# First loads of an attention-plus-MLP kernel: part of them moved to ScalarE's queue, the keys' tails multiplied last

## The chip, the cores and the metric

The kernel runs on one core of a Trainium2 chip. The metric is the device time of one execution in microseconds. An execution is one launch that computes the whole output from inputs in HBM.

## The reference, cut to what matters

There are 8 batches, 8 heads, 576 positions and a head size of 64. `phi` turns the 576 keys and values of a head into 32 "memory" keys and values; the queries attend to those; the result goes through an MLP from 512 to 2048 and back.

```python
a = phi - np.max(phi, axis=2, keepdims=True)
a = np.exp(a)
a = a / (np.sum(a, axis=2, keepdims=True) + 1e-09)
k_m = np.einsum('bhsm,bhsd->bhmd', a, k)
v_m = np.einsum('bhsm,bhsd->bhmd', a, v)
scores = (1.0 / np.sqrt(64)) * np.matmul(q, k_m.transpose(0, 1, 3, 2))
attn = np.exp(scores - np.max(scores, axis=-1, keepdims=True))
attn = attn / (np.sum(attn, axis=-1, keepdims=True) + 1e-09)
x = np.matmul(attn, v_m)        # then (B, S, H * D)
h = x @ w_in
out = (h - np.tanh(h)) @ w_out
```

## The kernel before, in words

The work is one long program written out in a fixed order. The text `START` is a list of words that the loop at its end runs one after the other; each word stands for a step in the table `STEPS`. Each engine then does its instructions strictly in the order of the words (`in_order` ties every instruction to the one ahead of it on its engine). The words of `START` prepare batch 0, convert the weights and lead into the steady part, which goes over 18 tiles of 256 tokens with 4 blocks of hidden units each.

The change touches the first words, those of batch 0:

- `FX0` loads `phi` (tile `pt`, two loads of 288 KB, one for each row of heads, `r` = 0 and 1).
- `KK01`, `KK00` load the keys of row 1 and row 0 (`load_half`, 520 KB each, tiles `kv01` and `kv00`, from `in_kk_dram`). With row 0 come the keys' tails, positions 512 to 575 (tile `kt`, 130 KB, from `in_kkt_dram`).
- `Q00`, `Q01` load the two halves of the queries (`load_q`, 576 KB each).
- `KV00`, `KV01` load the values of row 0 and row 1 (512 KB each, from `in_vv_dram`); with row 0 come the values' tails (128 KB, from `in_vvt_dram`).
- `XR`, `YX`, `XT` take each row's maximum of `phi` on VectorE (line 319), the exponential on ScalarE (line 322, in place in `pt`) and its transposes on TensorE (lines 335 and 336), whose results VectorE and ScalarE copy into tile `e`.
- `VK00`, `VK01` multiply `e` with the keys into `pk` on TensorE (`pool_first`, line 206 for the four full blocks, line 210 for the tails); `VV01`, `VV00` do it with the values later.
- `NK0`, `UK0`, `S00`, `S01`, `AM`, `AE`, `AD`, `AT` divide, transpose, make the scores and the softmax of batch 0.
- `Z00` is a warming pair, two matmuls of ones whose result nobody reads (`warm`, line 969). `N_WARM` such pairs stand ahead of all words.

A load is issued by an engine: SyncE (SP) for most, ScalarE (ACT) for the keys of row 0. The framework gives every load one of eight semaphores, `DMAHW0` to `DMAHW7`, in turn, and puts a wait on an issue that takes a semaphore for the second time: the load that had it before must have landed.

Of the kernel before, what the change touches and what calls it, by code (L numbers as in the profile page):

```python
# [62 lines left out]
        _free.append(P_TAG[_b, _f])  # L63

START = """
FX0 KK01 KK00 Q00 Q01 KV00 XR00 YX00 XT00 XR01 YX01 XT00 XT01 XT01 XT01 Z00 VK00 VK01 Z00 NK0 UK0 UK0 Z00 S00 Z00 S01
S00 AM00 S01 AM01 AM00 KV01 i4:kv2 i2:gg AM01 i3:gg AE00 VV01 Z00 i0:gg AD00 AE01 Z00 Z00 i1:pp5 Z00 VV00 Z00 T02 AD01
Z00 Z00 AD00 NV0 AT00 UU0 i6:kv3 T02 T01 T02 T01 T01 AD01 KB1 AT01 o0:pp5 T02 T00 T01 Z00 T00 L01 T00 T00 Lp02 Lp00
FX1 Lp00 o1:gg L01 UV0 Z00 T03 UV0 T03 T03 AS00 AS01 T03 o6:gg P00 AS00 P00 Lp03 PL00 Lp02 o7:gg Lp03 H00 AS01 P01 T08
H10 XR10 XR11 YX10 XT10 P01 H00 T08 PL01 ap00 YX11 KA1 o3:pp5 H10 o2:gg XT10 XT11 a10 XT11 ap00 T11 XT11 T11 T11 T08  # L70
# [24 lines left out]
N_PLACES = {"gg": 3, "h3": 2, "sm": 2, "sz": 2}  # L95
ENGINES = {name: row[0] for row in ENGINE_LIST.strip().splitlines() for name in row[2:].split()}
W_TAG = "qt us ot qt ot qt pr ot qt pr us ot qt us ot qt".split()
N_WARM = 5
N_CHECK = N_F1 + 2 * B + DF // P + DM // P


# [44 lines left out]
class Attention:  # L146
# [32 lines left out]
    def load_half(self, d, r, kv):  # L179

        n, o = ((65, 0), (64, 1040))[kv]
        src = self.ins[("kk", "vv")[kv]]
        if not kv:
            d["kv0", r] = self.big.tile([P, 2064], F32, tag=f"kv{r}", name=f"kv0{r}", bufs=1)
        t = d["kv0", r][:, o : o + 16 * n]
        queue = self.tc.nc.sync if kv or r else self.tc.nc.scalar
        queue.dma_start(t, src[r])
        for h in range(4):
            d["kv"[kv], h, r] = t.rearrange("p (h c x) -> p h c x", h=4, c=4)[:, h]
        if r == 0:  # L190
            if not kv:
                d["kt0"] = self.big.tile([P, 516], F32, tag="kt", name="kt0", bufs=1)
            t = d["kt0"][:, o // 4 : o // 4 + 4 * n]
            self.tc.nc.sync.dma_start(t, self.ins[("kkt", "vvt")[kv]])
            d["kv"[kv], "t"] = t.rearrange("p (h x) -> p h x", h=4)

    def pool_first(self, d, r, kv):

        nc, e, k = self.tc.nc, d["e"], "kv"[kv]
        if "pk" not in d:  # L200
            d["pk"] = self.psum("pk0")
        d[k, "p"] = pa = d["pk"][:, :, 128:192] if kv else d["pk"][:, :, 0:65]
        for c in range(4):
            for h in range(4):
                hs = slice(32 * h, 32 * h + 32)
                nc.tensor.matmul(pa[hs, r], e[:, c + 4 * r, hs], d[k, h, r][:, c], start=(c == 0), stop=False)
        rs = slice(64 * r, 64 * r + 64)
        for h in range(4):
            hs = slice(32 * h, 32 * h + 32)
            nc.tensor.matmul(pa[hs, r], e[rs, 8, hs], d[k, "t"][rs, h], start=False, stop=True)  # L210

    def norm_first(self, d, kv):
        nc, big, pa = self.tc.nc, self.big, d["kv"[kv], "p"]
# [37 lines left out]

    def load_q(self, b, d, t, tag):
        x = self.big.tile([P, 4, HS], F32, tag=tag, name=f"q{b}{t}", bufs=2 if tag == "q" else 1)
        self.tc.nc.sync.dma_start(x, self.ins["qt"][b, t])
        for h in range(4):
            d["q", h, t] = x[:, h]

# [203 lines left out]
def split_path(ctx, tc, c, ins, out, kept):  # L461
# [502 lines left out]
    def warm(*_):  # L964

        if "z" not in acc:
            acc["z"] = ps_o.tile([P, DM], F32, tag="o0", name="warm")
        for _ in range(2):
            nc.tensor.matmul(acc["z"], c["w16"], c["w16"].unsqueeze(1).to_broadcast((P, 4, P)), start=True, stop=True)
# [51 lines left out]

    for _ in range(N_WARM):
        warm()
# [380 lines left out]
```

## Time and profile before

| | |
|---|---|
| time, median of 3 runs | 639.83 us (639.36 to 640.59) |
| the profiled execution's own time | 639.59 us |
| its span, first to last instruction | 637.8 us |
| TensorE busy | 626.3 us, 98% of the span |
| VectorE, ScalarE, GpSimd busy | 514.8, 366.6, 276.1 us |
| chain of waits | 76% TensorE, 8% VectorE, 6% issue, 4% each GpSimd and ScalarE, 2% DMA |

The span is 1.79 us shorter than the execution's own time, and that execution is 0.24 us faster than the median. Nearly all of the span belongs to TensorE; the first 25 us are where it stands idle most.

### The profile page before, as it was taken

What the parts mean: (1) busy time and instruction counts of PE and PEld (TensorE: products, weight loads), DVE (VectorE), ACT (ScalarE), POOL (GpSimd) and SP (SyncE); (2) the same over time, 40 slices, a digit from 0 to 9 for tenths busy, and PEclk for the clock granted to TensorE, in tenths of its full rate; (3) what the DMA queues carried; (4) which work ended last, traced back from release to release, by engine and by line L of the source; (5) the groups of instructions that cost most, each with busy time, mean ns of one, the idle gap of its engine ahead of it and who ended that gap; (6) DMA issues with size and microseconds to landing.
All of it is one profiled execution on the core that took longest, in us unless ns stands there. A gap on an engine that the chain in (4) does not pass through costs nothing.

```text
span 637.8 us, 15488 instructions
## 1 busy us (share of the span) xinstructions
PE 626.3 (98%) x6656; PEld 452.4 (71%) x6656; DVE 514.8 (81%) x747; ACT 366.6 (57%) x487; POOL 276.1 (43%) x190
## 2 busy tenths in 40 slices
PE   7899999999999999999999999999999999999997
PEld 3374765556567778787867777778787777888886
DVE  5999888779995778875988889888987888858775
ACT  2777887544424555445564565645655576776641
POOL 2467665733042354423443363435432565455530
PEclk9999999999999999999999999999999999999999
DMA  8999750403232403243342432441353333234201
GB/s 337 363 351 412 273 208 34 141 1 134 69 115 105 170 3 108 37 161 136 108 101 93 174 100 55 148 175 39 104 158 142 101 120 113 83 108 126 83 35 38
DMA packets 28300, 85.50 MB, mean 134 GB/s; under 512 B 3648, under 2 KB 4416, under 8 KB 27712
## 3 DMA queue, kind: packets, MB, share of 16 engines
q1 hardware_dynamic: 26928, 81.80, 36.9%
q10 hardware_dynamic: 1296, 2.63, 1.1%
q8 instruction: 54, 0.88, 0.6%
q14 instruction: 22, 0.18, 0.1%
HBM read 72.88 MB, written 11.54 MB: 132 GB/s over the span
## 4 chain that ended last, share of the span: by engine, by line
PE 76%; DVE 8%; issue 6%; POOL 4%; ACT 4%; DMA 2%; POOLq 0%; ACTq 0%; DVEq 0%
PE hs L724 17%; PE x L871 12%; PE o L864 10%; PE o L805 9%; PE o L871 8%; PE h L724 7%; PE o1h L805 3%; PE pp L685 3%; PE pkv L355 2%; POOL g L760 2%; DVE h L749 2%; DVE f L773 2%; ACT u L731 2%; DVE h L739 2%; DMA kv<-in_kk_dram 1%
## 5 line engine op out<-in xcount | busy, mean ns | idle before, releaser
L760 POOL TENSOR_TENSOR g<-h,g 128x1024 f16<-128x1024 f32 x65 | 142.0, 2185 | 296.1 <-ACT g L114 198.7
L724 PEld LDWEIGHTS <-ph 128*128 128x128 f16 x2304 | 177.5, 98 | 18.8 <-issue 4.1
L724 PE MATMUL hs<-ah,ph 128*128 128x256 f16 (+3 forms) x1152 | 151.4, 246 | 0.0
L114 ACT ACTIVATE g<-h 128x1024 f16<-128x1024 f32 x69 | 73.0, 1057 | 102.9 <-DVE h L749 98.8
L724 PE MATMUL hs<-al,ph 128*128 128x256 f16 (+3 forms) x576 | 127.6, 246 | 0.0
L739 DVE SCALAR_TENSOR_TENSOR h<-hs,u 128x1024 f32<-128x1024 f32 x54 | 65.9, 1220 | 72.8 <-ACT u L731 72.1
L744 ACT ACTIVATE u<-u,beta 128x1024 f32<-128x1024 f32 x72 | 82.6, 1149 | 64.0 <-DVE h L739 64.0
L864 PE MATMUL o<-wout_hi,g 128*128 128x512 f16 x432 | 104.6, 379 | 0.0
L871 PEld LDWEIGHTS <-f 128*128 128x128 f16 x896 | 87.7, 98 | 10.1
L749 DVE SCALAR_TENSOR_TENSOR h<-u,h 128x1024 f32<-128x1024 f32 x72 | 88.2, 1226 | 3.5 <-ACT u L744 3.5
L871 PEld LDWEIGHTS <-g 128*128 128x128 f16 x672 | 64.1, 98 | 27.4 <-issue 6.0
L871 PE MATMUL x<-bt,f 128*128 128x256 f16 x672 | 82.5, 273 | 0.0
L731 ACT ACTIVATE u<-hs 128x1024 f32<-128x1024 f32 x54 | 54.8, 1016 | 28.0 <-PE hs L724 25.3
L773 DVE TENSOR_TENSOR f<-g 128x512 f16<-128x512 f16 x112 | 69.3, 659 | 1.7
L864 PEld LDWEIGHTS <-g 128*128 128x128 f16 x432 | 41.2, 98 | 40.2 <-issue 3.8
L805 PEld LDWEIGHTS <-g 128*128 128x128 f16 x384 | 36.6, 98 | 46.5 <-issue 2.6
L805 PE MATMUL o<-wout_hi,g 128*128 128x512 f16 x192 | 58.8, 379 | 0.0
L724 PE MATMUL h<-ah,ph 128*128 128x256 f16 (+3 forms) x384 | 50.0, 246 | 0.0
L724 PE MATMUL h<-al,ph 128*128 128x256 f16 (+2 forms) x192 | 42.5, 246 | 0.0
L805 PE MATMUL o<-wout_lo,g 128*128 128x512 f16 x96 | 36.4, 379 | 0.0
L703 DVE SCALAR_TENSOR_TENSOR ph<-pp,ph 128x1024 f16<-128x1024 f32 x26 | 31.6, 1217 | 4.0 <-ACT ph L114 4.0
L600 POOL TENSOR_TENSOR fy<-chk 128x512 f32<-128x512 f32 x32 | 33.7, 1067 | 0.0
(191 smaller groups left out, 968.7 us busy)
## 6 DMA issues: line engine op xcount, KB each, us to landing
q<-in_qt_dram SPq DMA_DIRECT2D x16, 576.0 KB, 5.6
kv<-in_kva_dram SPq DMA_DIRECT2D x16, 516.0 KB, 6.2
chk<-in_w_in_dram SPq DMA_DIRECT2D x16, 512.0 KB, 5.8
chk<-in_w_out_dram SPq DMA_DIRECT2D x16, 512.0 KB, 3.5
out_dram<-r SPq DMA_DIRECT2D x28, 256.0 KB, 2.4
raws<-in_w_in_dram SPq DMA_DIRECT2D x12, 511.8 KB, 8.3
raw<-in_w_out_dram SPq DMA_DIRECT2D x12, 511.8 KB, 6.6
kv<-in_kva_dram SPq DMA_DIRECT2D x4, 1032.0 KB, 10.3
```

The source lines that it names most:

```text
L114: nc.scalar.activation(o, x, AF.Copy, scale=1.0 if scale is None else scale)
L600: nc.gpsimd.tensor_tensor(y, hf, hf, op=ALU.mult)
L724: nc.tensor.matmul(hp[:, k, tu : tu + w], px[:, g, cs], d[ax][:, g, ta : ta + w], start=(n == 0), stop=(n == 5),)
L731: nc.scalar.activation(uu, hp, AF.Square, scale=1.0 / (S_A * S_P))
L739: nc.vector.scalar_tensor_tensor(h3, hp, C2 * S_G / (S_A * S_P), uu, op0=ALU.mult, op1=ALU.mult)
L744: nc.scalar.activation(uu, uu, AF.Square, bias=c["beta"])
L749: nc.vector.scalar_tensor_tensor(h3, uu, CC, hp, op0=ALU.add, op1=ALU.mult)
L760: (eng or on(nc, f"gl{u}_{fb}", "g")).tensor_tensor(gg[:, 1], h3, gg[:, 0], op=ALU.subtract)
L773: nc.vector.tensor_tensor(o, x, y, op=op)
L805: nc.tensor.matmul(o, gx[:, k, P * tt : P * tt + P], wx[:, 4 * fb + k, :], start=(first and k == 0 and wx is wout_hi and gx is gh), stop=( ...
L864: nc.tensor.matmul(o[th], gg[:, 0, k, P * th : P * th + P], wout_hi[:, 4 * fb + k, :], start=(first and k == 0), stop=False)
L871: nc.tensor.matmul(dst, a(1 - n, kk), b(n, kk), start=(new and kk == 0 and n == 0), stop=(end and kk == 1 and n == 1))
```

## The change

ScalarE's queue issues three more loads: the keys' tails, the second half of batch 0's queries, and the values of row 1. The word `KV01` goes from its place behind the first scores to the head of the list, so that its load is issued next to the others. In `pool_first` the products of the keys' tails for both rows come behind the full blocks of both rows (for the values nothing changes there). `N_WARM` goes from 5 to 6. Lines behind line 205 move by one or none: the exponential is line 323 now, the warming pair 970.

```diff
 START = """
-FX0 KK01 KK00 Q00 Q01 KV00 XR00 YX00 XT00 XR01 YX01 XT00 XT01 XT01 XT01 Z00 VK00 VK01 Z00 NK0 UK0 UK0 Z00 S00 Z00 S01
-S00 AM00 S01 AM01 AM00 KV01 i4:kv2 i2:gg AM01 i3:gg AE00 VV01 Z00 i0:gg AD00 AE01 Z00 Z00 i1:pp5 Z00 VV00 Z00 T02 AD01
+FX0 KK01 KK00 Q00 Q01 KV00 KV01 XR00 YX00 XT00 XR01 YX01 XT00 XT01 XT01 XT01 Z00 VK00 VK01 Z00 NK0 UK0 UK0 Z00 S00 Z00
+S01 S00 AM00 S01 AM01 AM00 i4:kv2 i2:gg AM01 i3:gg AE00 VV01 Z00 i0:gg AD00 AE01 Z00 Z00 i1:pp5 Z00 VV00 Z00 T02 AD01
-N_WARM = 5
+N_WARM = 6
@@ load_half
-        queue = self.tc.nc.sync if kv or r else self.tc.nc.scalar
-        queue.dma_start(t, src[r])
+        (self.tc.nc.scalar if kv == r else self.tc.nc.sync).dma_start(t, src[r])
-            self.tc.nc.sync.dma_start(t, self.ins[("kkt", "vvt")[kv]])
+            (self.tc.nc.sync if kv else self.tc.nc.scalar).dma_start(t, self.ins[("kkt", "vvt")[kv]])
@@ pool_first
-        rs = slice(64 * r, 64 * r + 64)
-        for h in range(4):
-            hs = slice(32 * h, 32 * h + 32)
-            nc.tensor.matmul(pa[hs, r], e[rs, 8, hs], d[k, "t"][rs, h], start=False, stop=True)
+        for i in (r,) if kv else range(2 * r):
+            rs = slice(64 * i, 64 * i + 64)
+            for h in range(4):
+                hs = slice(32 * h, 32 * h + 32)
+                nc.tensor.matmul(pa[hs, i], e[rs, 8, hs], d[k, "t"][rs, h], start=False, stop=True)
@@ load_q
-        self.tc.nc.sync.dma_start(x, self.ins["qt"][b, t])
+        queue = self.tc.nc.scalar if (b, t) == (0, 1) else self.tc.nc.sync
+        queue.dma_start(x, self.ins["qt"][b, t])
```

How this moves instructions is seen in the built programs. The rows below give source line, operation, written tile, read tiles and size; what stands in brackets are the semaphores that an instruction waits for (`DMAHW` of loads, the others of engines).

ScalarE's first instructions, before:

```order
L1345 ACT_TABLE_LOAD
L1345 ACTIVATE exp_66<-one_61 128x1 [waits Pool_49]
L187 DMA kv00_127<-in_kk_dram 128x1040
L322 ACTIVATE pt0_122<-pt0_122,mx00_137 128x576 [waits DMAHW0_49,DVE_49]
L322 ACTIVATE pt0_122<-pt0_122,mx01_148 128x576 [waits DMAHW1_49,DVE_49]
L114 ACTIVATE e0_141<-pet01_152 128x512 [waits PE_49]
```

and now:

```order
L1346 ACT_TABLE_LOAD
L1346 ACTIVATE exp_66<-one_61 128x1 [waits Pool_49]
L186 DMA kv00_129<-in_kk_dram 128x1040 [waits DMAHW0_49]
L193 DMA kt0_131<-in_kkt_dram 128x260 [waits DMAHW2_49]
L255 DMA q01_135<-in_qt_dram 128x1152 [waits DMAHW3_49]
L186 DMA kv01_127<-in_vv_dram 128x1024 [waits DMAHW5_49]
L323 ACTIVATE pt0_124<-pt0_124,mx00_140 128x576 [waits DVE_49]
L323 ACTIVATE pt0_124<-pt0_124,mx01_151 128x576 [waits DMAHW1_49,DVE_49]
L114 ACTIVATE e0_144<-pet01_155 128x512 [waits PE_49]
```

Ahead of the first exponential there were one issue and no wait for a load's semaphore but that of `phi`; now there are four issues, each with a wait for a semaphore of an earlier load.

SyncE's first issues, before:

```order
L164 DMA pt0_122<-in_phx_dram 128x576 x2
L187 DMA kv01_125<-in_kk_dram 128x1040
L194 DMA kt0_129<-in_kkt_dram 128x260
L254 DMA q00_131<-in_qt_dram 128x1152
L254 DMA q01_133<-in_qt_dram 128x1152
L187 DMA kv00_127<-in_vv_dram 128x1024
L194 DMA kt0_129<-in_vvt_dram 128x256 [waits DMAHW0_49]
L187 DMA kv01_125<-in_vv_dram 128x1024 [waits DMAHW1_49]
L494 DMA raws4_245<-in_w_in_dram 128x2047 [waits DMAHW2_49]
L494 DMA raws4_245<-in_w_in_dram 128x2047 [waits DMAHW3_49]
L494 DMA raw2_248<-in_w_in_dram 128x2047 [waits DMAHW4_49]
```

and now:

```order
L164 DMA pt0_124<-in_phx_dram 128x576 x2
L186 DMA kv01_127<-in_kk_dram 128x1040
L255 DMA q00_133<-in_qt_dram 128x1152
L186 DMA kv00_129<-in_vv_dram 128x1024
L193 DMA kt0_131<-in_vvt_dram 128x256
L495 DMA raws4_247<-in_w_in_dram 128x2047 x2
L495 DMA raw2_250<-in_w_in_dram 128x2047 [waits DMAHW1_49]
L495 DMA raw3_253<-in_w_in_dram 128x2047 [waits DMAHW4_49]
```

Three loads left SyncE's list. Its first eight loads now take the semaphores 0 to 7 in the order of the rows: `phi` 0 and 1, the keys of row 1 take 2, the first queries 3, the values of row 0 take 4, the values' tails 5, the first weights (`raws4`) 6 and 7.

TensorE's products with the keys (`pk0` is the accumulator), before:

```order
L206 MATMUL pk0_162<-kv00_127,e0_141 32x65 [waits DMAHW7_49,DVE_49]
L206 MATMUL pk0_162<-kv00_127,e0_141 32x65 x15
L210 MATMUL pk0_162<-kt0_129,e0_141 32x65 [waits DMAHW3_49,DVE_49]
L210 MATMUL pk0_162<-kt0_129,e0_141 32x65 x3
L206 MATMUL pk0_162<-kv01_125,e0_141 32x65 [waits DMAHW2_49,Activation_49]
L206 MATMUL pk0_162<-kv01_125,e0_141 32x65 x15
L210 MATMUL pk0_162<-kt0_129,e0_141 32x65 x4
```

and now, with the first rows of the scores (`psc00`, `psc01`) and of the products with the values behind them:

```order
L205 MATMUL pk0_165<-kv00_129,e0_144 32x65 [waits DMAHW0_49,DVE_49]
L205 MATMUL pk0_165<-kv00_129,e0_144 32x65 x15
L205 MATMUL pk0_165<-kv01_127,e0_144 32x65 [waits DMAHW2_49,Activation_49]
L205 MATMUL pk0_165<-kv01_127,e0_144 32x65 x15
L210 MATMUL pk0_165<-kt0_131,e0_144 32x65 [waits DMAHW2_49,DVE_49]
L210 MATMUL pk0_165<-kt0_131,e0_144 32x65 x7
...
L396 MATMUL psc00_219<-q00_133,kT0_215 32x288 [waits DMAHW3_49,Activation_49]
...
L396 MATMUL psc01_231<-q01_135,kT0_215 32x288 [waits DMAHW3_49]
...
L205 MATMUL pk0_165<-kv01_127,e0_144 32x64 [waits DMAHW5_49]
```

The eight tail products stand together behind the 32 others and the waits name the semaphores of the moved loads: tails 2, second queries 3, values of row 1 semaphore 5, each used a second time.

## Rows read from the trace of the kernel before

**Rows 1.** The page's parts 1 and 4: busy time, and the chain that ended last.

```profile
PE 626.3 (98%) x6656; PEld 452.4 (71%) x6656; DVE 514.8 (81%) x747; ACT 366.6 (57%) x487; POOL 276.1 (43%) x190
...
PE 76%; DVE 8%; issue 6%; POOL 4%; ACT 4%; DMA 2%; POOLq 0%; ACTq 0%; DVEq 0%
```

**Rows 2.** The chain in order of time, first 25 us: start us, us, what.

```profile
1.57 7.06 DMA kv<-in_kk_dram
8.63 0.14 issue
8.77 0.67 PE pk L206 x32
```

**Rows 3.** Timeline of ScalarE (ACT; ACTq is its sequencer): start us, us, what, idle before.

```profile
0.74 1.28 ACT L1345 ACT_TABLE_LOAD   x1 [0.74 <-PEq L1393]
1.57 0.41 ACTq L187 DMA_DIRECT2D kv<-in_kk_dram  x1
2.04 0.20 ACT L1345 ACTIVATE exp<-one 128x1 f32<-128x1 f32 x1
4.54 1.49 ACT L322 ACTIVATE pt<-pt,mx 128x576 f32<-128x576 f32 x2 [2.31 <-DVE mx L319]
```

**Rows 4.** Timeline of TensorE (PE).

```profile
1.06 3.95 PE L969 MATMUL warm<-w 128*128 128x512 f16 x10 [1.06 <-DVE w L1338]
5.42 0.63 PE L335 MATMUL pet<-ident,pt 128*128 128x128 f32 x4 [0.41 <-issue]
7.29 0.61 PE L969 MATMUL warm<-w 128*128 128x512 f16 x2
8.77 0.67 PE L206 MATMUL pk<-kv,e 128*32 128x65 f32 x32 [0.87 <-DMA kv<-in_kk_dram]
10.46 0.60 PE L969 MATMUL warm<-w 128*128 128x512 f16 x2
14.72 0.65 PE L206 MATMUL pk<-kv,e 128*32 128x64 f32 x32 [0.72 <-DMA kv<-in_vv_dram]
```

**Rows 5.** Timeline of SyncE's issues (SPq).

```profile
2.60 0.94 SPq L254 DMA_DIRECT2D q<-in_qt_dram  x2
3.07 0.47 SPq L254 DMA_DIRECT2D q<-in_qt_dram  x1
5.04 0.56 SPq L194 DMA_DIRECT2D kt<-in_vvt_dram  x1
8.84 0.82 SPq L494 DMA_DIRECT2D raws<-in_w_in_dram  x2
```

**Rows 6.** What SyncE's queue waited for, first 16 us: us in total, times, longest.

```profile
SPq L494 <- DMA kv<-in_kk_dram: 2.7, 1, 2.7
SPq L494 <- DMA q<-in_qt_dram: 1.8, 2, 1.1
```

**Rows 7.** Single issues in the DMA view: KB each, us from issue to landing.

```profile
q<-in_qt_dram SPq DMA_DIRECT2D x1, 576.0 KB, 7.8
q<-in_qt_dram SPq DMA_DIRECT2D x1, 576.0 KB, 8.7
kt<-in_vvt_dram SPq DMA_DIRECT2D x1, 128.0 KB, 8.4
```

**Rows 8.** Stretches: us, busy of PE, PEld, DVE, ACT, POOL, PEclk, DMA share, GB/s.

```profile
0.00:2.00 2.00, 0.94 (x3) 0.39 (x4) 0.82 (x3) 1.26 (x1) 1.39 (x12) 1.00 0.11 14
3.00:4.00 1.00, 1.00 (x3) 0.30 (x2) 0.76 (x3) 0.00 (x0) 0.37 (x1) 1.00 1.02 399
8.00:9.00 1.00, 0.23 (x17) 0.26 (x21) 0.00 (x0) 0.00 (x0) 0.00 (x0) 1.00 1.05 418
60.00:640.00 580.00, 572.69 (x6070) 423.48 (x6054) 465.03 (x673) 326.96 (x429) 247.73 (x157) 1.00 0.33 110
```

**Rows 9.** Warming matmuls of the first 5 us, then of 15 to 20 us: ns min/median/max.

```profile
L969 PE MATMUL warm<-w x10: 379/634/634, 1.1 to 4.6; 128*128 128x512 f16 x10
...
L969 PE MATMUL warm<-w x16: 379/379/390, 15.6 to 20.0; 128*128 128x512 f16 x16
```

## The prediction

> **What bounds the kernel now.** I read the page's busy shares and its chain first: TensorE is busy 98% of the span and holds 76% of the chain [rows 1]. The windows say where the other 2% are: from 60 to 640 us TensorE works 572.69 of 580 us [rows 8]. A delay that reaches this part can therefore not be caught up there, and a start that ends earlier is worth nearly its full length. So the question is what ends last in the start. The chain in order of time names it: ScalarE's issue of the keys of row 0 at 1.57, 7.06 us until they have landed at 8.63, and then at 8.77 the first product with the keys [rows 2]. TensorE's timeline agrees: it stood idle 0.87 us ahead of that product, waiting for the keys [rows 4]. Behind 8.77 the chain goes product, VectorE, GpSimd, ScalarE without a load in it, so each later step starts as much later or earlier as this product does.
>
> Two things beside the keys must be done before that product. ScalarE takes the exponentials of `phi` from 4.54 [rows 3]; TensorE's transposes of them start at 5.42, and the warming pair behind the transposes is done at 7.29 + 0.61 = 7.90 [rows 4]. So a product that waited for no load could start 7.90 - 4.54 = 3.36 us behind the start of the first exponential; in this run it had 0.87 us of slack.
>
> **The change part by part.**
>
> *Four issues ahead of the exponentials on ScalarE's queue.* In ScalarE's new list all four loads stand ahead of the first exponential, and each waits for a semaphore that another load used: the keys of row 0 for `phi`'s first load, the tails for the keys of row 1, the second queries for the first queries, the values of row 1 for the values' tails (semaphore 5, the sixth load of SyncE). Nothing in the data asks for that; it comes from eight semaphores going round. That such a wait does hold a queue is seen on SyncE: the weights' load shares no data with the keys, yet its issue stood 2.7 us until the keys of row 1 had landed and went out at 8.84, and two more issues stood 1.8 us behind the queries [rows 5, 6]. Now the same happens on a queue that has arithmetic behind it. The first exponential cannot start before the last of the four is issued, so before the values' tails have landed.
>
> When is that? I count the bytes that go ahead. Before, the first queries landed at 2.60 + 7.8 = 10.4 us with 2322 KB issued up to them, the second at 3.07 + 8.7 = 11.8 with 2898 KB, the values' tails at 5.04 + 8.4 = 13.4 with 3538 KB [rows 5, 7]. That is 1216 KB in 3.0 us, 405 KB in a microsecond, and the windows show the same, 399 to 418 GB/s with all 16 DMA engines busy [rows 8]. Now SyncE has 576 + 520 + 576 + 512 + 128 = 2312 KB up to the values' tails, and ScalarE's queue puts the keys of row 0 and the tails beside them, 650 KB: 2962 KB, which by those rows is 11.8 + 64 / 405 = 12.0 us. If nothing of ScalarE's queue went ahead, it is the 10.4 of 2322 KB; if the second queries went ahead too, it is the 13.4 of 3538 KB. I take 12.0, since ScalarE's two loads are issued early and its second queries only once the first ones are in. The last issue then takes 0.41 us as ScalarE's issue did [rows 3] and the wait some 0.1: the first exponential starts at **12.5 instead of 4.54**. Without a further cost the product starts at 12.5 + 3.36 = 15.9, which is **+7.1 us** against 8.77, between +5.5 and +8.5. Who waits behind it: VectorE's copies of `e`, GpSimd's subtraction of the maxima and SyncE's later loads into tiles that these steps free, all of them by as much.
>
> *TensorE's clock in the gap.* TensorE has nothing to do from the end of the warming pairs (1.06 + 3.95 = 5.0, some 0.4 later with the sixth) until its first transpose at about 13.4. In before it came out of an idle stretch once, at the start: of the first ten warming matmuls most lasted 634 ns, those of 15 to 20 us 379 [rows 9], though the granted-clock column prints 1.00 from the first row on [rows 8]. Ten in 3.95 us [rows 4] is 8 at about 0.43 and 2 at 0.22 apart, so it ran at the lower of its levels (1.2 GHz) first and lost 8 x 0.21 = 1.7 us there. No row shows whether it falls in a gap that comes later. The lower bound is nothing. The upper is that all of TensorE's work from the transposes through the products goes at half speed: (7.90 - 5.42) + (10.46 - 8.77) = 4.2 us more [rows 4]. I take the **1.7** of the start, as the engine comes out of idleness in both. The Trainium skill says (TensorE: Matmul & The Clock Gate, "What's actually happening") that the lower clock is the default and that activity lifts it; by that the term is there, without it the forecast would be 646.7. The start of this trace agrees with it, the gap has no row.
>
> *The tails' products behind the others.* The same 40 products in another order, none added: 0. They read the tails later, which helps only if the tails are the last to land. They are issued when the keys of row 1 have landed, and are among the 2962 KB that are in by 12.0; the products come behind 15.9.
>
> *Loads taken off SyncE.* SyncE reaches the weights sooner: its `raws4` issues wait for nothing now, where they went out at 8.84 [rows 5]. No step of the chain's first 16 us waits for weights, so this is worth 0. TensorE's 0.72 us at 14.72, the wait for the values of row 1 [rows 4], is not in the chain either, which goes over VectorE there; 0. The values of row 1 go out at 12.0 and are wanted some 8.8 us behind 14.72, at 23.5; the longest landing of the rows here is 8.7 [rows 7], which is covered.
>
> *The sixth warming pair.* Two more matmuls, at most 2 x 0.43 = 0.9 us on TensorE ahead of the transposes; the wait for the exponentials covers them. If that cover were gone they would end at 5.4 to 5.9 beside the transposes' 5.42, up to 0.5 us.
>
> **Sum** against the profiled execution's 639.59 us (0.24 below the median of the runs): +7.1 and +1.7 give +8.8, **648.4 us**. The ends of both terms give +5.5 (645.1) and +8.5 + 4.2 (652.3).
>
> **The rivals.**
>
> *The exponentials are not held (the other side).* Then the change does what its words say. The keys wait 0.87 us less, at most: the product starts at 7.90 and the time is 638.7. For it speaks that ScalarE's queue issued its load at 1.57 while its table load ran until 2.02 [rows 3]; issue and arithmetic do overlap. Against it: there the issue ran ahead of work that came earlier in the list; here the exponential would have to overtake an issue that waits. The point that decides is whether the first exponential starts at 4.5. And the tails would then land late, about 9.5 (130 KB behind 520 on ScalarE's queue, issued only when row 1's keys are in), so that most of the 0.87 is lost again: 638.7 to 639.6, or 638.0 at best if TensorE's 0.72 at 14.72 counted too. The Trainium skill goes further (DMA: Bandwidth & Descriptors, "Issuing engines are not separate DMA queues"): loads from several engines share the same 16 DMA engines, and spreading them saves only the time to issue. By that the gain would be nothing, 639.6; the rows with all DMA engines busy agree. Chance 0.04, a quarter of it for the best case.
>
> *Held, but for less.* The eight semaphores' waits end sooner than my count (the values' tails at 10.4 or before) and the clock does not fall: 639.59 + 5.5 = 645.1, or down to 643 if some of the delay is absorbed between 25 and 60 us by loads that are further ahead. No wait for a load stands in the chain there, so I give it 0.12.
>
> *Held, and the clock stays low through the products:* 639.59 + 7.1 + 4.2 = 650.9, or 652.3 with the late landing. Chance 0.14.
>
> *Something later takes all of the delay back,* so that nothing is seen: 639.6. The 572.69 of 580 us speak against it [rows 8]. Chance 0.01.
>
> **How the numbers follow.** The forecast has 0.69, with its own range 646.5 to 650. The range 644.6 to 651.5 takes in most of the two cases beside it and leaves out the not-slower ones and the farthest ends, some 0.12 together. A measurement of this kernel can tell 0.2% (1.3 us) from no change. Slower is all but the first and the last rival: 0.95; faster 0.01, the best case of the first rival; the same 0.04, the rest of it and the last rival.
>
> **What the changed profile would show.** Right: four issues on ScalarE's queue, the last at about 12 us; the first exponential at 12.5; the first product with the keys without a wait for a load, at 16 to 18; matmuls of 634 ns among the first behind the gap; and the same steps from there to the end, 8 to 9 us later. Wrong: an exponential at 4.5, a product with the keys ahead of 10 us, or a last issue on ScalarE's queue that starts early and waits for nothing.

## The result, and the profile after

The changed kernel took 649.25 us (median of 4 runs, 648.83 to 649.73) where the kernel before took 639.66 beside it (4 runs): a ratio of 1.0145, 95% interval 1.013 to 1.0159. It is slower by 9.6 us; the forecast was 648.4, the range 644.6 to 651.5. The profiled execution of the changed kernel took 648.83 us, its span is 647.0: 9.24 more than the profiled execution of before. It is the fastest of the four: its mean granted clock was 0.995, that of the other three 0.992.

The page of the changed kernel, parts 1 and 4, answers to [rows 1]: the chain lost 6 points of TensorE and gained 4 of VectorE and 2 of "issue".

```profile
PE 629.5 (97%) x6658; PEld 453.2 (70%) x6658; DVE 516.3 (80%) x747; ACT 366.1 (57%) x487; POOL 274.7 (42%) x190
...
PE 70%; DVE 12%; issue 8%; POOL 4%; ACT 4%; DMA 2%; SPq 0%; DVEq 0%; POOLq 0%; ACTq 0%
```

The chain in order of time shows the new hole, though not its cause: it calls it "issue", time in which TensorE waited for nothing that the profile shows.

```profile
1.06 5.30 PE warm L970 x12
6.36 6.84 issue
```

The cause stands in ScalarE's timeline of the changed kernel (against [rows 3]) and in two issues of its DMA view (KB each, us from issue to landing):

```profile
3.68 0.39 ACTq L186 DMA_DIRECT2D kv<-in_kk_dram  x1
6.52 0.34 ACTq L193 DMA_DIRECT2D kt<-in_kkt_dram  x1
8.71 0.33 ACTq L255 DMA_DIRECT2D q<-in_qt_dram  x1
11.95 0.33 ACTq L186 DMA_DIRECT2D kv<-in_vv_dram  x1
12.33 1.44 ACT L323 ACTIVATE pt<-pt,mx 128x576 f32<-128x576 f32 x2 [10.09 <-DMA kt<-in_kkt_dram]
```

```profile
kt<-in_vvt_dram SPq DMA_DIRECT2D x1, 128.0 KB, 8.9
kt<-in_kkt_dram ACTq DMA_DIRECT2D x1, 130.0 KB, 6.0
```

Four issues, each late by its semaphore, and then the exponentials at 12.33 instead of 4.54. The last issue went out at 11.95: the values' tails were issued at 3.07 and took 8.9 us to land. The exponentials' row names the keys' tails, the other load into tile `kt`; those landed only at 6.52 + 6.0 = 12.5, so the load that ended the wait is the values' tails. What follows on TensorE (against [rows 4]):

```profile
13.21 1.08 PE L336 MATMUL pet<-ident,pt 128*128 128x128 f32 x4 [6.84 <-issue]
17.36 1.13 PE L205 MATMUL pk<-kv,e 128*32 128x65 f32 x64
18.42 0.34 PE L210 MATMUL pk<-kt,e 64*32 64x65 f32 x16
18.70 0.60 PE L970 MATMUL warm<-w 128*128 128x512 f16 x2
```

The product with the keys starts at 17.36 instead of 8.77 and waits for no load. The windows of the changed kernel (columns as in [rows 8]) say that TensorE worked at half its clock there: 0.50 is 1.2 GHz.

```profile
10.00:12.00 2.00, 0.00 (x0) 0.00 (x0) 0.00 (x0) 0.00 (x0) 0.00 (x0) 0.59 1.05 393
12.00:17.00 5.00, 3.79 (x14) 2.14 (x14) 0.98 (x2) 2.04 (x3) 0.00 (x0) 0.50 1.02 414
17.00:18.00 1.00, 1.00 (x46) 0.64 (x48) 0.00 (x0) 0.00 (x0) 0.00 (x0) 0.91 1.01 410
```

To follow the delay further I take one late step of the start as a marker: GpSimd's second subtraction of the maxima in batch 0. In the kernel before:

```profile
16.05 1.16 POOL L425 TENSOR_TENSOR sc<-sc,sm 128x576 f32<-128x576 f32 x1 [0.31 <-DVE sm L423]
```

and in the changed one:

```profile
24.32 1.16 POOL L426 TENSOR_TENSOR sc<-sc,sm 128x576 f32<-128x576 f32 x1 [0.31 <-DVE sm L424]
```

The delay is 8.59 us at the first product, 8.27 at the marker (in the new order the products take 1.34 us, 17.36 to 18.70, where they took 1.69, 8.77 to 10.46 [rows 4]) and stays between 8.2 and 8.5 up to about 180 us. Then it grows by 0.73 in one place. VectorE's subtraction `bt` and GpSimd's subtraction `al` start within 20 ns of each other there, and one of them takes twice its time. In the kernel before, GpSimd's row and then VectorE's:

```profile
178.61 2.37 POOL L676 TENSOR_TENSOR al<-af,ah 128x576 f16<-128x576 f32 x1 [0.99 <-ACT ah L114]
...
178.63 1.21 DVE L787 TENSOR_TENSOR bt<-wout_lo 128x2048 f16<-128x2048 f16 x1
```

and the same two in the changed kernel:

```profile
187.02 1.28 POOL L677 TENSOR_TENSOR al<-af,ah 128x576 f16<-128x576 f32 x1 [0.99 <-ACT ah L114]
...
187.04 2.34 DVE L788 TENSOR_TENSOR bt<-wout_lo 128x2048 f16<-128x2048 f16 x1
```

I read the durations so: before, VectorE went first and GpSimd stood; now GpSimd went first and VectorE, which has more queued behind it, stood. From there the delay is 9.1 to 9.2 us to the end, but for single steps.

### The profile page after: what moved, and what is told of

The parts are those of the page before. It is cut to its first block, busy times and chain, and to the rows that moved or that the text cites. A ratio compares the mean times of both kernels' runs of the same rounds, so it can differ in the third digit from the quotient of the medians.

```text
span 647.0 us, 15491 instructions
## 1 busy us (share of the span) xinstructions
PE 629.5 (97%) x6658; PEld 453.2 (70%) x6658; DVE 516.3 (80%) x747; ACT 366.1 (57%) x487; POOL 274.7 (42%) x190
## 4 chain that ended last, share of the span: by engine, by line
PE 70%; DVE 12%; issue 8%; POOL 4%; ACT 4%; DMA 2%; SPq 0%; DVEq 0%; POOLq 0%; ACTq 0%
PE hs L725 16%; PE x L872 12%; PE o L865 9%; PE o L872 8%; PE h L725 6%; PE o L806 6%; PE o1h L806 3%; PE pp L686 2%; DVE h L750 2%; PE pkv L356 2%; DVE h L740 2%; DVE f L774 2%; ACT u L732 2%; POOL g L761 2%; DMA pt<-in_phx_dram 1%
## 5 line engine op out<-in xcount | busy, mean ns | idle before, releaser
L872 PE MATMUL o<-bt,g 128*128 128x256 f16 x224 | 33.6, 273 | 0.0
```

The costliest lines, as they stand in the source:

```text
L872: nc.tensor.matmul(dst, a(1 - n, kk), b(n, kk), start=(new and kk == 0 and n == 0), stop=(end and kk == 1 and n == 1))
```

## The experiments

Theory: ScalarE's queue is held by issues that wait for a reused semaphore, so the exponentials come late; the low clock behind the gap adds 1.7 us. Rivals: the loss comes from the loads as such (bytes on a second queue, another order of the transfers); it comes from the values of row 1 issued early, or from the order of the products; the low clock has no part in it. Each kernel ran beside the kernel before on one chip, and the ratios are to that.

**1. Only the three loads back on SyncE.** The other parts of the change stay.

```diff
-        (self.tc.nc.scalar if kv == r else self.tc.nc.sync).dma_start(t, src[r])
+        (self.tc.nc.sync if kv or r else self.tc.nc.scalar).dma_start(t, src[r])
-            (self.tc.nc.sync if kv else self.tc.nc.scalar).dma_start(t, self.ins[("kkt", "vvt")[kv]])
+            self.tc.nc.sync.dma_start(t, self.ins[("kkt", "vvt")[kv]])
-        queue = self.tc.nc.scalar if (b, t) == (0, 1) else self.tc.nc.sync
+        queue = self.tc.nc.sync
```

> The changed kernel with only its three extra loads of ScalarE's queue (keys' tails, second queries, values of row 1) put back on SyncE; the values of row 1 still early, the tails' products still last, the sixth warming pair still there. If the whole loss comes from ScalarE being held by waiting issues, the first exponential is back at about 4.5 us, the first product with the keys within 1 us of 8.8, and the time at 639.7, within 0.5 of the kernel before. If the early values of row 1 or the order of the products cost something by themselves, 641 to 649 remain.

Measured: 639.80 us, ratio 0.9998 (0.9984 to 1.0011). ScalarE's and TensorE's timelines:

```profile
4.46 1.47 ACT L323 ACTIVATE pt<-pt,mx 128x576 f32<-128x576 f32 x2 [2.22 <-DVE mx L320]
```

```profile
6.16 0.85 PE L336 MATMUL pet<-ident,pt 128*128 128x128 f32 x4
...
9.32 1.13 PE L205 MATMUL pk<-kv,e 128*32 128x65 f32 x64 [0.47 <-DMA kv<-in_kk_dram]
```

The three loads on ScalarE's queue are the whole loss. The early word `KV01`, the order of the products and the sixth pair cost nothing that can be measured. The order even gains: here too the products take 1.34 us (9.32 to 10.66) instead of 1.69, and the delay falls from 0.55 us at the product to 0.23 at the marker. The sixth pair does show: the twelve warming matmuls ended at 6.36, so the transposes stood until 6.16 instead of 5.42, and only the later landing of the keys covers that.

**2. One of the three loads at a time on ScalarE.** From the kernel of 1, one of its three edits is taken back at a time.

> Of the three loads only the keys' tails stay on ScalarE's queue. Its issue then waits for phi's second load alone. Held-by-waits: the first exponential starts at about 4.9 us (the landing of that load plus an issue), the slack of 0.87 us ahead of the product with the keys takes it up, and the time is that of the kernel before, 639.7 within 0.7. If it is the second queue's share of the DMA engines or its bytes that cost, the tails (130 of 1218 KB) cost a tenth of the loss, 0.9 us, which could hardly be told apart here; the place of the first exponential tells it.

Measured: 642.02 us, ratio 1.0031 (1.002 to 1.0043). The exponentials were where the theory has them, the time was not:

```profile
4.36 0.34 ACTq L193 DMA_DIRECT2D kt<-in_kkt_dram  x1
4.81 1.44 ACT L323 ACTIVATE pt<-pt,mx 128x576 f32<-128x576 f32 x2 [2.57 <-DVE mx L320]
```

```profile
11.03 0.35 PE L210 MATMUL pk<-kt,e 64*32 64x65 f32 x16 [1.05 <-DMA kt<-in_kkt_dram]
```

Issued at 4.36 instead of 2.12, the tails landed at 10.89, and even as the last products they had to wait: TensorE was through with them 0.85 us later than before (11.31 against 10.46). Behind this wait its clock column fell to 0.50 (12 to 14 us), and the delay was 1.93 us at the marker. That I had left out of the expectation. The clock also parts the twelve executions: the five with a mean granted clock of 0.999 or 1.0 took 640.08 to 641.36 us, the seven with 0.996 or 0.997 took 641.88 to 643.11.

> Of the three loads only the second queries stay on ScalarE's queue. By the semaphores their issue waits for the keys of row 1. Held-by-waits: that landing is at 6.5 to 7.0 us, the first exponential at 7.0 to 7.4, the product at 10.4 to 10.8, and the time 1.6 to 2.0 above the kernel before, 641.3 to 641.7 (up to 643 if TensorE's clock falls in its gap). If the loss goes with bytes on the second queue, 576 of 1218 KB cost 0.47 of 9.4 us: 644.1.

Measured: 644.73 us, ratio 1.0071 (1.0056 to 1.0087).

```profile
6.52 0.34 ACTq L255 DMA_DIRECT2D q<-in_qt_dram  x1
6.91 1.44 ACT L323 ACTIVATE pt<-pt,mx 128x576 f32<-128x576 f32 x2 [4.67 <-DMA kv<-in_kk_dram]
```

> Of the three loads only the values of row 1 stay on ScalarE's queue, early in the list. By the semaphores their issue waits for the keys of row 1, issued on SyncE ahead of two queries. Held-by-waits: that landing is at 7 to 8.9 us, the first exponential at 7.4 to 9.3, the product at 10.8 to 12.6, and the time 2 to 3.9 above the kernel before, 641.7 to 643.6, and up to 1.7 more if the clock falls. If the loss goes with bytes on the second queue, 512 of 1218 KB cost 0.42 of 9.4 us: 643.6; then the first exponential would still be at 4.5.

Measured: 645.16 us, ratio 1.0087 (1.0072 to 1.0102).

```profile
7.10 0.34 ACTq L186 DMA_DIRECT2D kv<-in_vv_dram  x1
7.54 1.44 ACT L323 ACTIVATE pt<-pt,mx 128x576 f32<-128x576 f32 x2 [5.31 <-DMA kv<-in_kk_dram]
```

In both, the exponentials start 0.4 us behind the late issue, and the row names the load whose semaphore it took: the keys, with which neither the queries nor the values share data. The place of the exponentials (4.81, 6.91, 7.54) goes by the semaphore, not by the bytes. The times alone would not tell the theories apart: 644.7 is above what holding gave for the queries and near the 644.1 of the bytes, 645.2 is at the upper end of holding for the values and above the 643.6 of the bytes. In the traces the rest is the clock: the column is 0.50 from 8 us on in the one and from 10 in the other, and the products started 5.14 and 4.17 us behind the exponentials instead of 3.36. The two profiled executions (643.33 and 642.77) are among the fastest of the timed ones, and no trace shows the others. For the values the record has a difference: a mean granted clock of 0.997 in the profiled execution, 0.994 or 0.995 in the four others (644.75 to 646.24 us). For the queries it has none that fits: 0.995 in the profiled one, 0.994 to 0.997 in the others.

**3. The same load on ScalarE's queue, behind the transposes.** From the third kernel of 2, one word is moved.

```diff
-FX0 KK01 KK00 Q00 Q01 KV00 KV01 XR00 YX00 XT00 XR01 YX01 XT00 XT01 XT01 XT01 Z00 VK00
+FX0 KK01 KK00 Q00 Q01 KV00 XR00 YX00 XT00 XR01 YX01 XT00 XT01 XT01 XT01 KV01 Z00 VK00
```

> As the run with the values of row 1 alone on ScalarE's queue, but their word stands behind the transposes of phi, so that the issue comes after ScalarE's copies of e, in a stretch where ScalarE has nothing to do, and waits there for a load that lands at 10 to 12 us. Held-by-waits: the same load on the same queue costs nothing: first exponential at 4.5, product with the keys within 0.8 of 8.8, time 639.7 within 1 (up to 1.5 more if the values of row 1 now land too late for their product). If it were the second queue's bytes, the 5.5 us above the kernel before that its twin showed would remain: 645.

Measured: 645.12 us, ratio 1.0077 (1.0064 to 1.009). That is the rival's number, by another way. The exponentials were at 4.39, as the theory says, and the product at 7.67, earlier than it says, but:

```profile
11.42 0.34 ACTq L186 DMA_DIRECT2D kv<-in_vv_dram  x1
11.80 0.28 ACT L114 ACTIVATE kT<-ptr 128x128 f32<-128x128 f32 x1 [4.32 <-DMA q<-in_qt_dram]
```

```profile
12.13 0.72 PE L396 MATMUL psc<-q,kT 64*32 64x288 f32 x16 [1.12 <-ACT kT L114]
...
19.10 1.08 PE L205 MATMUL pk<-kv,e 128*32 128x64 f32 x32 [5.07 <-DMA kv<-in_vv_dram]
```

The issue, now held until 11.42 by the queries' semaphore, took the copy of `kT` behind it along. That used up what the early product had gained and no more: the scores start at 12.13 against 12.10 before, the marker step at 16.08 against 16.05. The 5.5 us come behind it: the values landed at 19.06, 5.07 us after TensorE was ready, and its clock column stood at 0.50 from 18 to 24 us. So the run doesn't speak for the bytes, and the theory's expectation failed too: a held issue is paid for here as well, by the late landing of its own load.

**4. The three loads on GpSimd's queue.** GpSimd's three issues waited for no load in the trace (3.31, 4.03 and 4.55 us), and ScalarE has left only its one wait for `phi`.

```diff
-        (self.tc.nc.scalar if kv == r else self.tc.nc.sync).dma_start(t, src[r])
+        (self.tc.nc.scalar if kv + r == 0 else self.tc.nc.gpsimd if kv == r else self.tc.nc.sync).dma_start(t, src[r])
-            (self.tc.nc.sync if kv else self.tc.nc.scalar).dma_start(t, self.ins[("kkt", "vvt")[kv]])
+            (self.tc.nc.sync if kv else self.tc.nc.gpsimd).dma_start(t, self.ins[("kkt", "vvt")[kv]])
-        queue = self.tc.nc.scalar if (b, t) == (0, 1) else self.tc.nc.sync
+        queue = self.tc.nc.gpsimd if (b, t) == (0, 1) else self.tc.nc.sync
```

> The changed kernel with its three extra loads issued by GpSimd's queue instead of ScalarE's; the keys of row 0 stay on ScalarE and now wait for phi's first load. Held-by-waits: ScalarE issues that one load at about 3.7 us and the first exponential starts at 4.2 to 4.6; the keys of row 0 are issued 2.1 us later than before, so the product with the keys, or the tails' products behind it, start 0 to 2 us later than 8.8: 639.5 to 642. If taking the loads off SyncE, or the order in which they then share the DMA engines, were the loss, 649 would remain.

Measured: 646.27 us, ratio 1.0095 (1.008 to 1.0109), between the two answers. ScalarE's and TensorE's timelines, and the issue of the keys of row 0 in the DMA view:

```profile
3.66 0.38 ACTq L186 DMA_DIRECT2D kv<-in_kk_dram  x1
4.45 1.44 ACT L323 ACTIVATE pt<-pt,mx 128x576 f32<-128x576 f32 x2 [2.21 <-DVE mx L320]
```

```profile
12.94 1.96 PE L205 MATMUL pk<-kv,e 128*32 128x65 f32 x64 [5.14 <-DMA kv<-in_kk_dram]
```

```profile
kv<-in_kk_dram ACTq DMA_DIRECT2D x1, 520.0 KB, 9.1
```

There is a **second bound behind the hold**. The keys of row 0 are issued 2.1 us later, because they too wait for a semaphore, and by then SyncE has issued queries, values and tails and, at 3.54, the first of the weights, which in the kernel before went out at 8.84 [rows 5]: 9.1 us to landing instead of 7.06 [rows 2]. That the bytes ahead make the landing longer is my reading and not isolated: issued at 1.57 behind the same loads, the keys of row 0 took between 5.0 and 7.6 us in the kernel before, in that of 1, in the first and third of 2 and in that of 3. With the hold gone, 646.27 - 640.13 = 6.1 of the 9.6 us stay here. The low clock (0.50 from 11 to 17 us) and a lost tie are in them, and the changed kernel would keep less: there the keys of row 0 took 7.6 us and were in at 11.3.

**5. The hold alone.** The keys of row 0 go to SyncE, at once; the three loads stay on ScalarE.

```diff
-        (self.tc.nc.scalar if kv == r else self.tc.nc.sync).dma_start(t, src[r])
+        (self.tc.nc.scalar if kv and r else self.tc.nc.sync).dma_start(t, src[r])
```

> The changed kernel with the keys of row 0 also on SyncE, issued at once; the other three loads stay on ScalarE ahead of the exponentials. It takes apart the two things that kept the product back: ScalarE held, and the keys of row 0 issued late (3.7 us) among more bytes. By the semaphores ScalarE's last issue now waits for the first queries, which land at 10.0 to 10.4 us. If the hold by itself is a bound, the keys land by about 8 but the first exponential starts at 10.4 to 10.8, the product at 13.8 to 15.8 (with TensorE's clock), and the time is 644.7 to 646.7. If the late keys were the loss and the hold only went along with them, the product starts at 8.8 to 9.5 and the time is 639.7 to 640.4.

Measured: 645.97 us, ratio 1.0091 (1.0075 to 1.0106).

```profile
8.73 0.33 ACTq L186 DMA_DIRECT2D kv<-in_vv_dram  x1
9.11 1.44 ACT L323 ACTIVATE pt<-pt,mx 128x576 f32<-128x576 f32 x2 [6.88 <-DMA kv<-in_kk_dram]
```

```profile
14.25 1.69 PE L205 MATMUL pk<-kv,e 128*32 128x65 f32 x64
```

The product waits for no load, so the hold is a bound by itself. I had named the wrong load: the semaphore belongs here to the keys of row 0, in at about 8.7, not to the first queries, so the exponential came 1.3 us ahead of what I expected. That product and time still fit comes from the clock: 5.14 us from exponential to product.

**6. TensorE kept busy in the gap.** 22 warming pairs instead of 6 in the changed kernel.

```diff
-N_WARM = 6
+N_WARM = 22
```

> The changed kernel with 22 warming pairs instead of 6, which fill TensorE's empty stretch up to about 12.3 us; nothing else differs. If the clock costs what I booked for it, the granted clock stays at 1.00 through the transposes, the product with the keys starts 3.4 us behind the first exponential instead of 5.0, at 15.7, and the time is 647.6, 1.7 below the changed kernel's 649.25. If the low clock costs nothing that lasts, the product may start earlier but the time stays at 649.3.

Measured: 647.52 us, ratio 1.011 (1.0096 to 1.0125). TensorE's timeline, and one window:

```profile
1.06 11.86 PE L970 MATMUL warm<-w 128*128 128x512 f16 x44 [1.06 <-DVE w L1339]
...
15.88 1.13 PE L205 MATMUL pk<-kv,e 128*32 128x65 f32 x64
```

```profile
12.00:17.00 5.00, 4.45 (x91) 2.56 (x94) 0.98 (x2) 2.04 (x3) 0.00 (x0) 1.00 1.03 416
```

The granted clock stays at 1.00 where it was 0.50; the product comes 3.28 us behind the first exponential (12.60) instead of 5.03, although that exponential came 0.27 later. The median is 1.73 us below the changed kernel's; against the kernels before beside them it is 7.4 us of loss instead of 9.6, and between the profiled executions 1.37 us.

**7. All first loads on SyncE, keys first.** A try to beat both kernels: ScalarE issues nothing, the keys go ahead of the queries, the products' order of the change stays, five pairs.

```diff
-FX0 KK01 KK00 Q00 Q01 KV00 KV01 XR00
+FX0 KK00 KK01 Q00 Q01 KV00 KV01 XR00
-N_WARM = 6
+N_WARM = 5
-        (self.tc.nc.scalar if kv == r else self.tc.nc.sync).dma_start(t, src[r])
+        self.tc.nc.sync.dma_start(t, src[r])
```

(the other two loads as in 1)

> All first loads on SyncE in the order phi, keys of row 0, tails, keys of row 1, queries, values; ScalarE issues none; tails' products last as in the change, five warming pairs as before. Held-by-waits: the first exponential at 4.5 us. The keys then have no query load ahead of them; if they land by 7.9 the product starts there and the time is 0.9 below the kernel before, 638.8; if one queue alone brings them later (before, ScalarE's load went beside SyncE's), the product starts at 8 to 9.5 and the time is 639 to 640.4.

Measured: 639.77 us, ratio 0.9996 (0.9987 to 1.0005). The product fits the first answer, the time the second. TensorE got its gain and lost it again, as its timeline and ScalarE's show:

```profile
7.59 0.67 PE L205 MATMUL pk<-kv,e 128*32 128x65 f32 x32
8.76 0.67 PE L205 MATMUL pk<-kv,e 128*32 128x65 f32 x32 [0.50 <-DMA kv<-in_kk_dram]
```

```profile
17.85 1.38 ACT L114 ACTIVATE tops<-raws 128x1024 f16<-128x1024 bf16 x1 [0.72 <-DMA raws<-in_w_in_dram]
...
20.35 0.79 ACT L114 ACTIVATE tops<-raw 128x512 f16<-128x512 bf16 x1 [0.50 <-DMA raw<-in_w_in_dram]
```

The marker step was at 15.25, 0.80 earlier than before, but ScalarE then waited for the weights, and of the 0.80 us 0.43 was left in this execution (639.16). The windows of this kernel show a DMA share of 0.95 or more in every stretch from 5 to 19 us, so I take it that the weights could come earlier only with something else coming later.

**8. The tie of VectorE and GpSimd taken away**, in the changed kernel and in that of 7: the word `G21` goes behind two other steps of VectorE.

```diff
-G21 R3 KR30 ap41 PL23 AS21 ap41 c40 AS21 O3 c41 F40 O3
+R3 KR30 ap41 PL23 G21 AS21 ap41 c40 AS21 O3 c41 F40 O3
```

> The changed kernel with one word (G21, VectorE's subtraction bt) moved behind the two VectorE steps that followed it, so that it does not start within 20 ns of GpSimd's subtraction al any more; the start is unchanged. If the two engines exclude each other there and the tie went the wrong way in the changed kernel, bt takes 1.2 us instead of 2.34, the delay behind that place is 8.4 us and not 9.15, and the time is 648.5. If the later delay comes from elsewhere, 649.25 remains.

Measured: 649.28 us, ratio 1.0143 (1.0125 to 1.0162): the 0.7 us do not show. The place did what was expected; GpSimd's row and then VectorE's:

```profile
188.12 1.28 POOL L677 TENSOR_TENSOR al<-af,ah 128x576 f16<-128x576 f32 x1 [0.98 <-ACT ah L114]
...
190.60 1.22 DVE L788 TENSOR_TENSOR bt<-wout_lo 128x2048 f16<-128x2048 f16 x1
```

Neither is lengthened, and the delay is 9.5 us in front of this place and behind it. But it was already 9.52 at the marker step (25.57), where the changed kernel had 8.27: the low clock lasted longer in this execution, and the first products took 1.96 us instead of 1.13. All four executions of this kernel had a mean granted clock of 0.992, like all of the changed kernel's but the profiled one. So what the tie is worth in the median stays open.

> The kernel with all first loads on SyncE and five warming pairs, with the word G21 moved as in the run before. Its profiled execution had the tie the good way, so the trace should hardly change; if some of the timed executions had it the bad way, 0.73 us each, the median falls by 0 to 0.7, to 639.0 to 639.8, and the executions lie closer together. If the weights' loads bound the start, as the trace of that kernel says (ScalarE waited for them at 17.85 and 20.35), no more than that is to be had.

Measured: 639.79 us, ratio 0.9998 (0.9989 to 1.0008): the upper end of the expectation, no gain that can be measured, and executions hardly closer together (639.36 to 641.31 against 639.06 to 641.42). Neither kernel beats the one before.

All profiled executions side by side (times in us; delay is the marker step's start less 16.05; the last column is the execution's own time less 639.59):

| kernel | first exponential | product with the keys | delay at the marker | VectorE lost the tie | time |
|---|---|---|---|---|---|
| before | 4.54 | 8.77 | 0 | no | 0 |
| 1, loads back | 4.46 | 9.32 | 0.23 | yes | 0.91 |
| 2, tails | 4.81 | 8.85 | 1.93 | yes | 2.57 |
| 2, values | 7.54 | 11.71 | 3.23 | no | 3.18 |
| 2, queries | 6.91 | 12.05 | 3.81 | no | 3.74 |
| 4, GpSimd | 4.45 | 12.94 | 5.52 | yes | 6.45 |
| 5, hold alone | 9.11 | 14.25 | 5.72 | yes | 6.48 |
| 6, clock kept | 12.60 | 15.88 | 6.78 | yes | 7.87 |
| changed | 12.33 | 17.36 | 8.27 | yes | 9.24 |
| 8, changed, no tie | 12.51 | 17.65 | 9.52 | none | 9.59 |
| 3, values behind the transposes | 4.39 | 7.67 | 0.03 | no | 5.53 |
| 7, all on SyncE | 4.31 | 7.59 | -0.80 | no | -0.43 |
| 8, that of 7, no tie | 4.39 | 7.67 | -0.68 | none | 0.39 |

The last three have a wait behind the marker (the values at 19.10; the weights, at 17.85 and 20.35 in 7), so it does not hold their delay. In the ten others: where VectorE won the tie or there was none, the time is the delay at the marker within 0.1 us; where it lost, the time is 0.6 to 1.1 more. Nothing between 25 us and the end took a delay back.

## Why the prediction was right, point by point

**The hold: right in place and size, the size partly by luck.** Forecast: last issue at 12.0, first exponential at 12.5, product +7.1. Measured: 11.95, 12.33, and 12.33 + 3.36 - 8.77 = +6.9. Experiments 2 and 5 show the cause: the exponentials follow the landing of a load that shares nothing with them but a semaphore. The count behind the 12.0 did not hold in its parts: the keys of row 0 and the keys' tails were not issued early but at 3.68 and 6.52, both behind the values' tails (3.07); the keys' tails were in only at 12.5; and two loads of the weights, of which it counts no byte, went out between 3.58 and 5.0.

**The clock: right.** Forecast +1.7 between 0 and 4.2; the changed kernel's trace gives 5.03 - 3.36 = 1.67, experiment 6 gives 1.73 in the medians (1.4 to 2.2 by the other comparisons). The sign of 634 ns came near: behind the gap two warming matmuls took 524 and 609 ns, and the transposes 421 ns instead of 272. The Trainium skill's rule that the lower clock is the default and activity lifts it (TensorE: Matmul & The Clock Gate, "What's actually happening") now has its row in this trace: 0.50 behind the gap, 1.00 with the gap filled. But the size was a fortunate choice within its bounds: in the first kernel of 8 the low clock lasted through the products and cost about 1 us more.

**Loads taken off SyncE: booked at nothing, and wrong.** I had written that the weights, issued earlier, are worth 0. Experiment 4 shows their price: together with the late issue of the keys they bring the keys of row 0 in at 12.80; no run parts the two. I had listed that issue's wait for `phi` and booked no cost for it. In the changed kernel both lie under the hold (the keys were in at 11.3, the product could not start before 15.7), which is why the sum came out right.

**The first rival was therefore mis-priced.** "Not held" would not have given 638.0 to 639.6: experiment 4, which is not held, took about 646, and even with the landing of the changed kernel (11.3) the product would have started some 2.6 us late, an estimate. The Trainium skill's rule beside it (DMA: Bandwidth & Descriptors, "Issuing engines are not separate DMA queues") is that loads from several engines share the same DMA engines and a second one saves only the time to issue. The runs agree: no kernel with loads on a second queue, that of before included, was measurably faster than that of 7, which has one.

**The tails' products last: booked at 0, a gain of 0.35 us.** In the changed kernel they wait for nothing, and the same products take 1.34 us instead of 1.69; the rows do not show why. With the tails issued 2.2 us later (the first kernel of 2) even the last place left 1.05 us of waiting.

**The sixth pair: 0, right; its bound was short.** Uncovered it would cost 6.16 - 5.42 = 0.74 us, not up to 0.5.

**Nothing is taken back later: right, and a term was missing.** The sum of +8.8 stood at +8.6 at the first product, at 8.27 at the marker and at 8.41 in front of the tie (178.61 to 187.02); the lost tie, which I had not looked for, then added 0.73 in the profiled execution. That this execution ends 0.4 us from the forecast owes something to two terms that I did not have and that go against each other, -0.35 and +0.73. The 0.85 us between forecast and median stay open: the tie may be in them, but the kernel without the tie took the same 649.28, and the other three executions, which lift the median above the profiled one, had a lower mean granted clock (0.992 against 0.995).

## What to carry to other kernels

Before a load is moved to the queue of an engine that computes, read which semaphores its issue waits for, and what stands behind it in that engine's list: a wait in an issue holds the arithmetic behind it, and the load that it waits for may have nothing to do with either. When a bound is found, price the next one behind it too, by taking the first away: in experiment 4 the keys' later landing, with the low clock behind it, kept 6.1 of the 9.6 us. With the DMA engines full (a share of 0.95 or more in 7), loads issued earlier did not all land earlier: the weights there went out at 6.83 instead of 8.84 and were still waited for at 17.85. So ask which bytes the first step needs, and let those go first.

## What the runs showed of the hardware that was not expected

VectorE and GpSimd excluded each other in one place of every traced execution in which the two subtractions stood side by side, eleven of them, and there were two outcomes: `bt` 1.21 and `al` 2.37 us, or 2.33 to 2.34 and 1.28. In both, GpSimd's record starts 20 to 30 ns ahead, so no row shows what settles it; it can add 0.7 us some 170 us behind the place that was changed. The Trainium skill states the mechanism (SBUF — State Buffer, "SBUF: two separate sides"): the two engines share a port pair that one of them holds for a whole instruction, and VectorE needs it for two operands in SBUF. The rows agree: the step of VectorE that ran beside `al` in the first kernel of 8, one of whose operands is an accumulator of TensorE, took its usual 1.22 us. By the Trainium skill's page the engine that starts first has the ports; the records, with GpSimd ahead in both outcomes, do not show that.

The low clock does not last equally long in executions that start alike: the first products with the keys took 1.13 us in the changed kernel, whose column was back at 0.91 between 17 and 18 us, and 1.96 in the first kernel of 8, whose products began 0.3 us later and whose column stayed at 0.50 up to 20 us.
